# The small constant of sixty softmax sums: added by VectorE in front of its reciprocal instead of by ScalarE

## The chip, the cores and the metric

The kernel runs on one core of one Trainium2 chip. The metric is the device time of one launch in microseconds (us), given as the median of several runs of the same program.

## What is computed

A causal attention over 4 batches and 12 heads (448 positions, head dimension 64) is followed by a gated feed-forward block with an RMS norm in front of it. Cut to what matters here:

```
scores = q @ k^T / 8, causal mask, minus the row maximum
attn   = exp(scores)
attn   = attn / (sum(attn) + 1e-9)          # this sum and this 1e-9
x      = attn @ v                           # heads side by side, 1792 tokens by 768
xn     = x / sqrt(mean(x * x) + 1e-6) * g
out    = (silu(xn @ w_gate) * (xn @ w_val)) @ w_out
```

## The kernel before

The attention is cut into 60 units: a pair of heads (one head on each half of the partitions) times a block of queries. The first 12 units (kind 0) have 256 queries as two blocks, so each has four softmax sums per partition; the other 12 of the first two groups look the same, and the last 36 (kinds 1 and 2) have two sums per partition. The feed-forward block runs in between: its matmuls for the first groups of tokens lie among the attention's steps, so that TensorE has work while a softmax is under way.

Each engine works through its own instructions in the order in which the program was written. That order comes from a hand-made clock: `tick()` counts steps, `post(delay, fn)` writes an instruction so many steps later, and the table `T` holds the delays. Nothing is moved by a scheduler, so an instruction that waits holds everything behind it on its engine.

One unit p goes through these steps:

- **Scores** (L193): TensorE multiplies queries and keys into a PSUM bank.
- **Masked maximum** (L202): VectorE adds the mask, scales, writes the tile `sp` and gets the row's extreme `nm`. That is one custom instruction and one that reads its accumulator, for each head and block.
- **Exponential** (L205): ScalarE takes exp of `sp` in place and gets the row sum `sm` through its accumulator.
- **The constant** (L227): one ScalarE Identity with a bias tile `tiny` of 1e-9 adds the constant to all two or four sums of the unit in place.
- **Reciprocal** (L214, in `norm`): VectorE writes `rs` from `sm`. A pair of units that is treated in one round has its two reciprocals side by side.
- **Normalization** (L210 on GpSimd, called POOL in the profile; L208 on ScalarE for units 10 to 23): `sp` times `rs`.
- **Transposes** (L249) by TensorE, **copies** to `pt` (L253 by VectorE, L255 by ScalarE), and the **product with v** (L275) by TensorE into `a_ps`, which L292 copies out.

Between these, VectorE and ScalarE also prepare the weights of the feed-forward block. ScalarE scales a weight tile (L414) and rounds it to a high part `w_h` (L429); VectorE puts together bit fields (L417 and then L419, which reads what L417 wrote) and takes the low part `w_l` (L431). Later VectorE forms sums of weight tiles (L450). POOL takes a share of this too (L415, L103).

Of the kernel before, what the change touches and what calls it, by code (L numbers as in the profile page):

```python
# [10 lines left out]
F32 = mybir.dt.float32  # L11
# [4 lines left out]
AF = mybir.ActivationFunctionType  # L16
# [6 lines left out]
P = 128  # L23
# [15 lines left out]
        for g in range(NG) for c in range(NP)}  # L39
ENDS = [max(i for i, u in enumerate(UNITS) if u[0] == g) + 1 for g in range(NG)]  # L40
# [3 lines left out]
T = dict(c0=0, c1=1, c10=5, c2=4, c20=16, c3=4, c30=18, c26=5, c36=5, c5=6, c50=19, c56=7, exp=1, exp0=3, gt=1, hh=1, hl=4, ws=5, ld2=7,  # L44
         ld=4, ld1=11, lv=5, norm0=7, norm1=2, r0=1, acc=10, acc4=7, dg=1, spread=2, r1=5, so=3, wl=2, wl0=7, wl2=5, wl4=1, xl=2, xl0=9)
# [17 lines left out]
def attention_ffn(ctx: ExitStack, tc: tile.TileContext, qk0, qk1, qk2, v, v2, w, g, out, out2):  # L63
# [7 lines left out]
    nc = tc.nc  # L71
# [3 lines left out]
    def pool(name, bufs, at=ctx, **kw):  # L75
        return at.enter_context(tc.tile_pool(name=name, bufs=bufs, **kw))

    const = pool("const", 1, side="left")
# [15 lines left out]
    def bank(tag, bufs=1):  # L94


        return ps.tile([P, W], F32, tag=tag, name=tag + "_ps", bufs=bufs)
# [22 lines left out]
    nc.vector.memset(ones, 1.0)  # L120
    eps = const.tile([P, 1], F32, name="eps")
    nc.vector.memset(eps, 1e-6)
    tiny = const.tile([P, 1], F32, name="tiny")
    warm_up = const.tile([P, 1], F32, name="warm_up")
    nc.vector.memset(tiny, 1e-9)
    g_sb = const.tile([P, KD], F32, name="g_sb")


# [3 lines left out]
    def post(delay, fn):  # L132
        if delay <= 0:
            fn()
        else:
            later.setdefault(now[0] + delay, []).append(fn)
# [14 lines left out]
    def load_qk(p):  # L151
        if p < len(UNITS):
            _, kind, _, _, row, _ = UNITS[p]
            raw_qk[p] = raw.tile([P, 2, W], F32, tag="qk", name="qk_r")
            if kind == 2:
                nc.sync.dma_start(out=raw_qk[p], in_=qk2[row])
            else:
                nc.sync.dma_start(out=raw_qk[p][:, 0], in_=(qk0, qk1)[kind][row])
# [10 lines left out]
    def blocks(kind):  # L169

        return [(0, P), (P, 2 * P)] if kind == 0 else [(0, KEYS[kind])]

    def steps_s(p):


        if not 0 <= p < len(UNITS):
            return []
        _, kind, _, _, _, _ = UNITS[p]
        pr = hs[p] = dict(norms=[])
        bl = blocks(kind)  # L180
        nb = 2 * len(bl)

        def scores(pss):
            for i, (o, wd) in enumerate(bl):
                for h in range(1 + (kind == 2)):
                    for e in range(2):
                        r = raw_qk[p][e * D: (e + 1) * D, h]
                        if kind == 2:
                            ps, q0, nq = pss[e][h * D: (h + 1) * D, :wd], 0, D
                        else:  # L190
                            ps, q0, nq = pss[e][:, o: o + wd], i * P, P
                        k0 = nq if kind else 2 * P
                        nc.tensor.matmul(ps, r[:, q0: q0 + nq], r[:, k0: k0 + wd],  # L193
                                         start=True, stop=True)

        def softmax(e, i, pss):
            o, wd = bl[i]
            ps, sp = pss[e][:, o: o + wd], pr["sp"][e][:, o: o + wd]
            n = len(bl) * e + i
            nm, sm, rs = (pr[m][:, n: n + 1] for m in ("nm", "sm", "rs"))  # L200
            mk = mask2 if kind == 2 else mask[:, 3 * P - wd:]
            nc.vector.tensor_tensor_reduce(  # L202
                out=sp, in0=ps, in1=mk, scale=nsc, scalar=3.0e38,
                op0=ALU.add, op1=ALU.min, accum_out=nm)
            post(T["exp" if p >= ENDS[0] else "exp0"], lambda: nc.scalar.activation(  # L205
                sp, sp, AF.Exp, bias=nm, scale=-1.0, accum_out=sm))
            if ENDS[0] - 2 <= p < ENDS[1]:
                pr["norms"].append(lambda: nc.scalar.mul(sp, sp, rs))  # L208
            else:
                pr["norms"].append(lambda: nc.gpsimd.tensor_scalar(  # L210
                    sp, sp, rs, 1.0, op0=ALU.mult, op1=ALU.mult))

        def norm():
            nc.vector.reciprocal(pr["rs"][:, :nb], pr["sm"][:, :nb])  # L214
            post(2 if ENDS[0] - 2 <= p < ENDS[0] else 0, lambda: [f() for f in pr["norms"]])

        def step():
            for nm in ("nm", "sm", "rs"):
                pr[nm] = st_p.tile([P, 4], F32, tag=nm, name=nm)
            pr["sp"] = [sp_p.tile([P, S], F32, tag="sp", name="sp") for _ in range(2)]  # L220
            pss = [bank(t_) for t_ in "xy"] if p > ENDS[1] + DP and p % 2 == 0 else [
                bank("s", 2) for _ in range(2)]
            scores(pss)
            for e in range(2):
                for i in range(len(bl)):
                    softmax(e, i, pss)
            post(T["exp" if p >= ENDS[0] else "exp0"], lambda: nc.scalar.activation(  # L227
                pr["sm"][:, :nb], pr["sm"][:, :nb], AF.Identity, bias=tiny))
            post(T["norm1" if kind else "norm0"], norm)
            post(2, lambda: load_qk(p + 4))  # L230

        return [step]
# [602 lines left out]
    with tc.manual_schedule():  # L835
# [157 lines left out]
        for q in range(21):  # L993
            i, p = divmod(q, 3)
# [58 lines left out]
```

## Time and profile before

| | |
|---|---|
| Median of 3 runs | 682.22 us (682.05 to 683.24) |
| The profiled execution | 681.84 us, of which the span of all instructions is 680.0 us |
| TensorE (PE) busy | 667.7 us, 98% of the span |
| VectorE (DVE) busy | 535.2 us, 79% |
| ScalarE (ACT) busy | 378.3 us, 56% |
| GpSimd (POOL) busy | 287.7 us, 42% |
| Granted TensorE clock | 1.00 in every stretch, which is the upper of its two levels |

Busy times are sums over instructions. The shares are averages over stages that differ much: in the first 50 us attention runs almost alone, from 68 us on the feed-forward matmuls fill TensorE, and from 428 us on there is no attention any more. The durations of neighbouring VectorE or ScalarE instructions overlap a little in the records, so the distance from one start to the next says what an instruction costs its engine. In the rows, "idle" is the time an engine stood still in front of an instruction, and the name behind the arrow is what ended it.

### The profile page before, as it was taken

The page shows a single profiled execution, that of the slowest core. Times are in us where ns is not written, and L with a number is a line of the kernel's source. Part 1 is how long each engine was busy: PE and PEld are TensorE (multiplying, and loading weights), DVE is VectorE, ACT ScalarE, POOL GpSimd, SP SyncE. Part 2 cuts the span into 40 slices and gives each one's busy share as a digit, 9 for nine tenths or more (in the row PEclk, how much of TensorE's full clock was granted, in tenths as well). Part 3 has the DMA queues.
Part 4 walks back from the last instruction along what each step waited for, and adds up shares of the span by engine and source line. Part 5 has one row for each costly group of instructions (what it writes and reads, how often), then busy time and mean ns, then how long its engine had stood idle before and what let it go on. Part 6 is the DMA issues. An engine that isn't in the chain of part 4 may idle for free.

```text
span 680.0 us, 11926 instructions
## 1 busy us (share of the span) xinstructions
PE 667.7 (98%) x4116; PEld 550.8 (81%) x4116; DVE 535.2 (79%) x1059; ACT 378.3 (56%) x855; POOL 287.7 (42%) x262
## 2 busy tenths in 40 slices
PE   8989999999999999999999999999999999999997
PEld 5566877777777767777777777888999999999997
DVE  4998998999888486877777878487577866889982
ACT  6986779787876444545545353434534343355540
POOL 4971121222235427565765665563333342402220
PEclk9999999999999999999999999999999999999999
DMA  8765788787977556777667645316775457563541
GB/s 269 243 235 189 230 244 291 230 262 242 283 260 283 164 159 233 216 242 207 228 213 239 208 159 182 122 62 197 250 242 178 161 194 240 196 172 89 155 140 59
DMA packets 71356, 138.81 MB, mean 204 GB/s; under 512 B 7744, under 2 KB 39232, under 8 KB 71296
## 3 DMA queue, kind: packets, MB, share of 16 engines
q1 hardware_dynamic: 71296, 138.05, 63.0%
q8 instruction: 33, 0.54, 0.3%
q14 instruction: 27, 0.22, 0.1%
HBM read 104.21 MB, written 33.82 MB: 203 GB/s over the span
## 4 chain that ended last, share of the span: by engine, by line
PE 68%; DVE 1%; ACT 1%; DMA 0%; issue 0%; SPq 0%; DVEq 0%; ACTq 0%
PE s_ps L625 10%; PE m_ps L475 9%; PE m_ps L625 9%; PE m_ps L477 9%; PE m_ps L476 9%; PE y_ps L625 5%; PE a_ps L275 5%; PE x_ps L625 4%; PE t_ps L249 4%; PE s_ps L193 2%; PE x_ps L193 2%; DVE w_r L450 1%; DMA w_o<-wsum 0%; ACT sp L205 0%; ACT w_c L414 0%
## 5 line engine op out<-in xcount | busy, mean ns | idle before, releaser
L475 PE MATMUL m_ps<-xh,w_h 128*128 128x512 f32 x276 | 117.3, 425 | 0.0
L210 POOL TENSOR_SCALAR sp<-sp,rs 128x384 f32<-128x384 f32 (+2 forms) x112 | 77.7, 711 | 90.7 <-DVE rs L214 86.1
L205 ACT ACTIVATE sp<-sp,nm 128x384 f32<-128x384 f32 (+3 forms) x168 | 87.1, 521 | 41.3 <-DVE nm L202 41.3
L477 PE MATMUL m_ps<-xh,w_l 128*128 128x512 f32 x276 | 108.4, 393 | 0.0
L476 PE MATMUL m_ps<-xl,w_h 128*128 128x512 f32 x276 | 108.3, 392 | 0.0
L415 POOL TENSOR_SCALAR w<-w 128x768 f32<-128x768 f32 x36 | 39.8, 1108 | 104.4 <-ACT w_c L414 98.3
L103 POOL TENSOR_TENSOR a_l<-w_q,a_h 128x768 fp32r<-128x768 f32 x24 | 48.2, 2007 | 81.0 <-ACT a_h L516 81.0
L275 PEld LDWEIGHTS a_ps<-pt,v_r 128*64 128x64 f32 (+1 forms) x864 | 42.1, 137 | 31.9 <-issue 9.7
L275 PE MATMUL a_ps<-pt,v_r 128*64 128x128 f32 (+2 forms) x864 | 58.5, 268 | 6.0 <-DVE pt L253 3.2
L103 POOL TENSOR_TENSOR w_l<-w_r,w_h 128x768 fp32r<-128x768 f32 x30 | 59.5, 1992 | 6.2 <-ACT w_h L429 6.0
L475 PEld LDWEIGHTS m_ps<-xh,w_h 128*128 128x128 f32 x276 | 51.9, 188 | 11.8 <-issue 3.7
L477 PEld LDWEIGHTS m_ps<-xh,w_l 128*128 128x128 f32 x276 | 51.9, 188 | 11.8
L253 DVE COPY pt<-t_ps 128x384 f32<-128x384 f32 (+1 forms) x71 | 42.4, 597 | 23.9 <-PE t_ps L249 23.5
L475 PE MATMUL m_ps<-hh,w_h 128*128 128x512 f32 x144 | 58.6, 407 | 0.0
L202 DVE CUSTOM_DVE_ANT_0 sp<-s_ps,mask 128x128 f32<-128x128 f32 (+3 forms) x136 | 49.7, 414 | 10.9 <-PE s_ps L193 9.9
L476 PEld LDWEIGHTS m_ps<-xl,w_h 128*128 128x128 f32 x276 | 52.2, 189 | 7.6
L477 PE MATMUL m_ps<-hh,w_l 128*128 128x512 f32 x144 | 56.3, 391 | 0.0
L476 PE MATMUL m_ps<-hl,w_h 128*128 128x512 f32 x144 | 56.2, 390 | 0.0
L249 PE MATMUL t_ps<-ident,sp 128*128 128x128 f32 (+1 forms) x309 | 50.1, 275 | 0.1
L249 PEld LDWEIGHTS t_ps<-ident,sp 128*128 128x128 f32 (+1 forms) x309 | 37.9, 138 | 14.3 <-issue 2.0
L193 PE MATMUL s_ps<-qk_r 64*128 64x128 f32 (+3 forms) x296 | 42.6, 425 | 0.5 <-DVE nm L202 0.4
L516 ACT CAST a_h<-w_q 128x768 fp32r<-128x768 f32 (+1 forms) x48 | 35.0, 754 | 14.1 <-DMA w_q<-wz 4.3
(194 smaller groups left out, 1667.9 us busy)
## 6 DMA issues: line engine op xcount, KB each, us to landing
w<-in_w SPq DMA_DIRECT2D x36, 768.0 KB, 5.7
w<-w_c SPq DMA_DIRECT2D x36, 384.0 KB, 5.8
w_r<-w SPq DMA_DIRECT2D x36, 384.0 KB, 4.5
qk_r<-in_qk SPq DMA_DIRECT2D x48, 256.0 KB, 4.6
qk_r<-in_qk SPq DMA_DIRECT2D x12, 512.0 KB, 5.7
v_r<-in_v SPq DMA_DIRECT2D x12, 448.0 KB, 4.8
v_r<-in_v SPq DMA_DIRECT2D x24, 192.0 KB, 3.0
wy<-w_r SPq DMA_DIRECT2D x24, 192.0 KB, 4.3
```

The source lines that it names most:

```text
L103: nc.gpsimd.tensor_tensor(out_, a, b, op=op)
L193: nc.tensor.matmul(ps, r[:, q0: q0 + nq], r[:, k0: k0 + wd], start=True, stop=True)
L202: nc.vector.tensor_tensor_reduce(out=sp, in0=ps, in1=mk, scale=nsc, scalar=3.0e38, op0=ALU.add, op1=ALU.min, accum_out=nm)
L205: post(T["exp" if p >= ENDS[0] else "exp0"], lambda: nc.scalar.activation(sp, sp, AF.Exp, bias=nm, scale=-1.0, accum_out=sm))
L210: pr["norms"].append(lambda: nc.gpsimd.tensor_scalar(sp, sp, rs, 1.0, op0=ALU.mult, op1=ALU.mult))
L249: nc.tensor.transpose(ps[:kb, at: at + P], pr["sp"][e][:, o + kb * j: o + kb * (j + 1)], ident)
L253: nc.vector.tensor_copy(pt[:kb, :at], ps[:kb, :at])
L275: nc.tensor.matmul(av_ps[e * D: (e + 1) * D, p % 2, q0: q0 + n], raw_v[p][:kb, h, j, e, :], pr["pt", e][:kb, a0: a0 + n], start=(j == 0), ...
L475: nc.tensor.matmul(ps, wh[:, k, :], mh, start=(first and k == ks[0]), stop=False)
L476: nc.tensor.matmul(ps, wh[:, k, :], ml, start=False, stop=False)
L477: nc.tensor.matmul(ps, wl[:, k, :], mh, start=False, stop=(last and k == 5))
L625: nc.tensor.matmul(ps, a[x], b[y], start=first and n == 0, stop=last and n == 2, skip_group_check=True)
```

## The change

The Identity on ScalarE goes away, with its bias tile `tiny` and the memset that fills it. In its place `norm` begins with a VectorE instruction that writes `sm + 1e-9` to `rs`, and the reciprocal then reads `rs` and writes it again in place.

```
-    tiny = const.tile([P, 1], F32, name="tiny")
     warm_up = const.tile([P, 1], F32, name="warm_up")
-    nc.vector.memset(tiny, 1e-9)
...
         def norm():
-            nc.vector.reciprocal(pr["rs"][:, :nb], pr["sm"][:, :nb])
+            nc.vector.tensor_scalar_add(pr["rs"][:, :nb], pr["sm"][:, :nb], 1e-9)
+            nc.vector.reciprocal(pr["rs"][:, :nb], pr["rs"][:, :nb])
...
-            post(T["exp" if p >= ENDS[0] else "exp0"], lambda: nc.scalar.activation(
-                pr["sm"][:, :nb], pr["sm"][:, :nb], AF.Identity, bias=tiny))
```

On VectorE, in the stretch of kind 0 units, this stood behind the maxima of one unit before (square brackets name the engines whose semaphores the instruction waits for, here Activation for ScalarE and DVE for VectorE itself):

```order
L202 ISA nm 128x1
L214 RECIPROCAL rs<-sm 128x4 [waits Activation_49]
L292 COPY xr<-a_ps 128x256 [waits PE_49]
L431 TENSOR_TENSOR w_l<-w_c,w_h 128x768 [waits Activation_49]
L253 COPY pt<-x_ps 128x384 [waits PE_49]
```

With the change the same place reads as follows, with line numbers that are lower by two or three:

```order
L200 ISA nm 128x1
L212 TENSOR_SCALAR rs<-sm 128x4 [waits Activation_49]
L213 RECIPROCAL rs<-rs 128x4 [waits DVE_49]
L289 COPY xr<-a_ps 128x256 [waits PE_49]
L428 TENSOR_TENSOR w_l<-w_c,w_h 128x768 [waits Activation_49]
L250 COPY pt<-x_ps 128x384 [waits PE_49]
```

The wait for ScalarE moved to the added instruction, and the reciprocal now waits for VectorE's own instruction in front of it. The order of all the rest is the same on VectorE.

On VectorE, in the rounds of two units late in the attention, two reciprocals stood side by side before:

```order
L253 COPY pt<-t_ps 112x512 [waits PE_49]
L214 RECIPROCAL rs<-sm 128x2 [waits Activation_49] x2
L502 TENSOR_TENSOR t_sb<-t_sb,m_ps 128x512 [waits PE_49]
L253 COPY pt<-t_ps 112x512 [waits PE_49]
L450 TENSOR_TENSOR w_r<-w_r 128x384 [waits DMAHW2_49,DVE_49]
```

With the change there are four small instructions, each reciprocal behind the add that it needs:

```order
L250 COPY pt<-t_ps 112x512 [waits PE_49]
L212 TENSOR_SCALAR rs<-sm 128x2 [waits Activation_49]
L213 RECIPROCAL rs<-rs 128x2 [waits DVE_49]
L212 TENSOR_SCALAR rs<-sm 128x2 [waits Activation_49]
L213 RECIPROCAL rs<-rs 128x2 [waits DVE_49]
L499 TENSOR_TENSOR t_sb<-t_sb,m_ps 128x512 [waits PE_49]
```

There are 16 such pairs and 28 single places, 60 adds in all, and 60 Identities and one memset fewer. The orders of TensorE, of POOL and of the queue that issues the transfers are the same as before.

## Rows read from the trace of the kernel before

**Rows 1.** Busy time of each engine by stretch (us, instructions in brackets).
```profile
core 0: us, PE busy (x) PEld busy (x) DVE busy (x) ACT busy (x) POOL busy (x), PEclk, DMA share, GB/s
17.00:51.00 34.00, 30.29 (x205) 19.63 (x204) 33.05 (x103) 31.90 (x103) 28.67 (x37) 1.00 0.70 239
...
68.00:402.00 334.00, 333.56 (x2171) 252.18 (x2169) 273.66 (x584) 207.63 (x507) 150.05 (x139) 1.00 0.72 232
...
428.00:605.00 177.00, 177.00 (x956) 167.52 (x955) 126.44 (x189) 71.88 (x124) 69.88 (x42) 1.00 0.56 185
```

**Rows 2.** Waits of TensorE: us in total, times, longest.
```profile
PE a_ps L275 <- DVE pt L253: 3.2, 6, 1.3
PE a_ps L275 <- DMA v_r<-in_v: 1.8, 2, 1.0
...
PE a_ps L275 <- ACT pt L255: 0.9, 4, 0.3
```

**Rows 3.** Groups of ScalarE: busy us, mean ns, idle before.
```profile
L227 ACT ACTIVATE sm<-sm,tiny 128x2 f32<-128x2 f32 (+1 forms) x60 | 17.8, 297 | 1.9
```

**Rows 4.** Timeline of ScalarE around one Identity: start us, duration us.
```profile
22.64 0.19 ACT L205 ACTIVATION_READ_ACCUMULATOR sp<-sp,nm 128x1 f32 x1
22.74 0.50 ACT L205 ACTIVATE sp<-sp,nm 128x256 f32<-128x256 f32 x1
23.14 0.19 ACT L205 ACTIVATION_READ_ACCUMULATOR sp<-sp,nm 128x1 f32 x1
...
23.56 0.82 ACT L429 CAST w_h<-w_c 128x768 fp32r<-128x768 f32 x1
```

**Rows 5.** Small VectorE instructions, groups by shape: busy us, mean ns.
```profile
L214 DVE RECIPROCAL rs<-sm 128x2 f32<-128x2 f32 x36 | 4.1, 150 | 3.9 <-ACT sm L227 3.9
...
L358 DVE TENSOR_SCALAR dg<-ident,rc 128x128 f32<-128x128 f32 x4 | 0.9, 283 | 0.1
...
L122 DVE MEMSET eps<- 128x1 f32 x1 | 0.1, 59 | 0.0
```

**Rows 6.** Timeline of VectorE, an instruction and one that reads its result.
```profile
59.75 0.95 DVE L417 SCALAR_TENSOR_TENSOR w<-w 128x768 int32<-128x768 int32 x1
60.73 0.96 DVE L419 SCALAR_TENSOR_TENSOR w_c<-w_c,w 128x768 int32<-128x768 int32 x1
```

**Rows 7.** Timeline of VectorE, 14 to 50 us, idle time in square brackets.
```profile
14.83 0.18 DVE L214 RECIPROCAL rs<-sm 128x4 f32<-128x4 f32 x1 [1.48 <-ACT sm L227]
...
17.28 0.18 DVE L214 RECIPROCAL rs<-sm 128x4 f32<-128x4 f32 x1 [0.40 <-ACT sm L227]
...
20.62 0.18 DVE L214 RECIPROCAL rs<-sm 128x4 f32<-128x4 f32 x1 [0.25 <-ACT sm L227]
...
28.03 0.17 DVE L214 RECIPROCAL rs<-sm 128x4 f32<-128x4 f32 x1
...
49.23 0.96 DVE L431 TENSOR_TENSOR w_l<-w_c,w_h 128x768 fp32r<-128x768 f32 x1 [0.41 <-ACT w_h L429]
```

**Rows 8.** Reciprocals from 20.6 to 49 us: durations, first and last start.
```profile
L214 DVE RECIPROCAL rs<-sm x8: 161/166/179, 20.6 to 48.3; 128x4 f32<-128x4 f32 x8
```

**Rows 9.** Timeline of TensorE where it stood still for a copy.
```profile
54.03 1.31 PE L275 MATMUL a_ps<-pt,v_r 128*64 128x256 f32 x8 [0.20 <-ACT pt L255]
...
107.39 0.86 PE L275 MATMUL a_ps<-pt,v_r 128*64 128x256 f32 x6 [0.18 <-ACT pt L255]
...
200.02 0.86 PE L275 MATMUL a_ps<-pt,v_r 128*64 128x256 f32 x6 [0.25 <-ACT pt L255]
...
414.64 0.87 PE L275 MATMUL a_ps<-pt,v_r 128*64 128x128 f32 x10 [0.48 <-DVE pt L253]
```

**Rows 10.** Chain that ended last, two stretches: start us, us on the chain.
```profile
192.16 0.10 DVE rs L214
...
197.39 0.03 ACT sm L227
...
408.55 0.14 DVE rs L214 x2
```

**Rows 11.** Timeline of POOL.
```profile
27.66 1.03 POOL L103 TENSOR_TENSOR sq<-xr 128x512 f32<-128x512 f32 x1
```

## The prediction

> **What bounds the kernel now.** I read the busy time by stretch first. From 428 us on TensorE has no gap and there is no softmax left, so nothing of the change can act there except by shifting the whole tail [rows 1]. From 68 to 402 us TensorE works 333.56 of 334.00 us, while VectorE is free for 60.3 us and ScalarE for 126 us [rows 1]. From 17 to 51 us it is otherwise: VectorE is busy for 33.05 of 34 us, ScalarE for 31.90, and TensorE stands still for 3.7 us [rows 1]. So I looked at TensorE's waits next. It waits 3.2 us for copies that VectorE makes of transposed weights of attention, in 6 places, and 0.9 us for those of ScalarE [rows 2]. A change that touches VectorE and ScalarE can move the end only where TensorE stands still for one of them, and TensorE's gaps then say by how much. They lie in three places: the stretch up to 54 us, two single gaps of 0.18 and 0.25 us at 107 and 200 us, and one of 0.48 us at 414.6 us [rows 9]. The chain that ended last agrees for the last two: it goes through VectorE's reciprocals at 192.16 and 408.55 us and through one Identity at 197.39 us [rows 10].
>
> **What the removal gives.** 60 Identities of 297 ns go, 17.8 us of busy time [rows 3]. On its engine one costs less or more than its duration, so I take distances between starts: from the last accumulator read to the next work is 0.42 us with an Identity between (23.14 to 23.56), and 0.10 us without (22.64 to 22.74), which makes 0.32 us [rows 4]. The sum itself is ready about 0.33 us sooner: the read at 23.14 ends at 23.33, and with the Identity the result would come at some 23.66 us (23.56, its successor's start, plus the 0.10 us by which neighbours overlap). The memset of 59 ns runs once, before TensorE has scores [rows 5].
>
> **What the addition costs.** The trace has no VectorE add on four columns, so I bound it. The reciprocal on two columns takes 150 ns, a scalar operation on 128 columns 283 ns, and a memset of one column 59 ns [rows 5]. The add is nearest to the reciprocal: same input memory, same output, as few columns. I take 0.15 us, with 0.06 and 0.28 us as ends. The reciprocal must now wait until the add is finished. What such a wait adds is shown by L417 and L419: the first ends at 60.70 us and the second, which reads its result, starts at 60.73 us, so 0.03 us [rows 6]. One add thus costs VectorE S = 0.18 us in front of the reciprocal, with bounds of 0.09 and 0.31 us. Nothing behind the reciprocal changes.
>
> The Trainium skill, "VectorE: DVE Perf Modes", section on the TRN2 errata, gives 58 cycles plus the columns for an operation from SBUF to SBUF, which would make an estimate of 0.06 us for the add, S = 0.09 us, and a sum at the low end below; the same section says that its own measurements have a fixed part of about 150 cycles, an estimate of 0.16 us. By the reciprocal's 150 ns the trace agrees with the second.
>
> **First place, up to 54 us: +0.34 us.** Three reciprocals stand behind ScalarE: VectorE waits 1.48, 0.40 and 0.25 us at 14.83, 17.28 and 20.62 us [rows 7]. There the add lies partly in time that was lost anyway. Each such place gains 0.33 - 0.18 = 0.15 us at most; three in a row could add up to 0.45 us, but the gain is cut where the copies behind them wait for transposes, so I take 0.30 us in the middle. From 20.6 us on VectorE works without a gap until 48.8 us. Eight reciprocals lie there, the first being the one just counted [rows 8]. The other seven put 7 x 0.18 = 1.26 us in front of everything behind them: the copy of `a_ps`, the work on weights, and the copy L253 for which TensorE waits. That leaves VectorE 1.26 - 0.30 = 0.96 us late. At 49.23 us it stood 0.41 us waiting for `w_h` from ScalarE [rows 7], and ScalarE, which there has one Identity less in front of it, doesn't get later by as much; the wait takes up 0.41 us, and 0.55 us is left. At 54.03 us TensorE had waited 0.20 us for a copy by ScalarE [rows 9]; that takes up 0.20 us more. Left: 0.34 us. With S = 0.31 the three places give nothing, seven adds cost 2.17 us, and 1.56 us is left. With S = 0.09 VectorE is 0.50 us ahead after the third place, pays 0.63 us, and the rest is decided by ScalarE's own chain, which has lost an Identity: about -0.25 us. TensorE's two waits for `v_r`, 1.8 us [rows 2], lie in the same stretch; they could swallow a gain, not a loss, since the copies arrive about when these transfers do.
>
> **Second place, 107 and 200 us: -0.30 us.** The ScalarE work that ends in the copy has one Identity in it and one reciprocal ahead of it (192.16 and 197.39 us in the second case [rows 10]). Each gives 0.18 - 0.33 = -0.15 us, which both gaps have room for [rows 9]. Bounds: -0.42 us, where the first gap is used up, and -0.04 us.
>
> **Third place, 408 to 415 us: +0.36 us.** The pair of reciprocals at 408.55 us lies on the chain [rows 10]; behind it come the evicted product, a tanh on ScalarE, weight sums and the copy for which TensorE waits at 414.64 us [rows 9]. Two adds make 0.36 us (0.18 to 0.62), and that gap grows by it.
>
> **Everywhere else: 0.** Of the 48 adds after 64 us, 8.6 us of work, all but the few above fall into VectorE's 60.3 us of free time [rows 1]. Where that cover fails, a pair costs TensorE 0.36 us. ScalarE's 15 us of saved work there fall into its 126 us of free time.
>
> **The sum.** 0.34 - 0.30 + 0.36 = +0.40 us, between -0.5 and +2.1 us. On the profiled execution this makes 682.24 us (681.84 + 0.40). The median of the runs shown is 0.38 us above that execution, so the forecast for a median is 682.22 + 0.40 = 682.6 us. A measurement of this kernel can tell about 0.2%, 1.36 us, from no change, so this is no change.
>
> **Rival: VectorE's add waits for POOL, slower.** If the add may not run while POOL is in an instruction of its own, VectorE stands still until POOL is through. The reciprocal at 28.03 us shows what is at stake: POOL runs from 27.66 to 28.69 us [rows 7, 11], so an add there would start 0.66 us late. POOL is busy for 28.67 of the 34 us [rows 1]. Were six of the nine adds from 17 us on caught, each for some 0.5 us, 3.0 us would come on top: 685.6 us. It decides as soon as two or three adds are caught. For it: VectorE has no gap there that could cover it. Against it: a scalar operation on 128 columns takes only 133 ns more than a reciprocal on two [rows 5], which is near one column a cycle, so the form seen here doesn't seem to run in a faster mode.
>
> The Trainium skill, "SBUF — State Buffer", section "Who interferes with whom", has the rule behind this: a scalar operation on VectorE can enter a mode that uses two ports, one pair of which it shares with GpSimd, and then whichever comes second waits for the whole instruction. By that rule the time would be the 685.6 us above if the mode is entered, and the forecast's if not; no row here shows the add's mode.
>
> **Rival: ScalarE sets the pace up to 50 us, faster.** If the two engines run in step because VectorE's work waits on ScalarE's, then eight rounds give 0.32 us each: -2.6 us in the first place, -2.5 us in all, 679.7 us. For it: three waits of VectorE for an Identity, and ScalarE busy for 31.90 of 34 us [rows 1, 7]. Against it: behind 20.62 us the reciprocals never wait again, as only the first of the eight in that stretch has a wait.
>
> That the change doesn't do what it says is excluded by the order of instructions: the Identities are gone and the adds stand in front of the reciprocals.
>
> **How the numbers follow.** The forecast has a chance of 0.72, the wait for POOL 0.15, ScalarE's pace 0.07, and 0.06 is for a loss beyond 1.36 us without POOL: S at its upper end (+2.1 us), or a few more pairs that are not covered. Faster by over 0.2%: 0.07. Within: 0.72. Slower: 0.15 + 0.06 = 0.21. The range goes from 681.5 us (the sum's low end, 681.7, and a spread of the runs) to 684.6 us (its high end, 684.3, and the same); it leaves out the faster case and most of the wait for POOL.
>
> **What would show it.** In the profile after, the distance from the start of an add to that of its reciprocal should be 0.18 us; much more, and unequal, where POOL is at work means the first rival. VectorE's waits before the sums at 14.8 to 20.6 us should be shorter by about 0.3 us each, TensorE's gaps at 107 and 200 us nearly closed, that at 414.6 us about 0.8 us. TensorE should come to its first work after 54 us some 0.3 us later than before. If it gets there over 1 us earlier, ScalarE set the pace and the prediction is wrong; if over 1.5 us later, the adds cost more than any small row of the trace says.

## The result, and the profile after

The changed kernel takes 685.39 us (median of 6 runs, 685.07 to 686.5), the kernel before 682.13 us beside it (6 runs, 679.74 to 683.24). The ratio is 1.0062, with an interval of [1.0048, 1.0076]: slower, by 3.3 us from median to median and by some 4 us by the ratio. The prediction said 682.6 us, in a range from 681.5 to 684.6 us. The time lies above that range, and beside the 685.6 us of the first rival, the wait of VectorE's add for POOL.

The profiled execution took 686.02 us, its span 684.2 us. First the busy time by stretch, with the same columns as [rows 1]:

```profile
17.00:51.00 34.00, 29.88 (x190) 18.71 (x191) 33.73 (x112) 26.96 (x88) 29.80 (x41) 0.95 0.58 198
68.00:402.00 334.00, 333.64 (x2169) 251.67 (x2168) 281.06 (x630) 197.51 (x465) 149.93 (x133) 1.00 0.73 232
```

From 17 to 51 us ScalarE has 4.94 us less to do than in [rows 1] and VectorE 0.68 us more, and TensorE starts 190 matmuls in place of 205. The stretch holds less work and VectorE is as full as before, so something in it takes VectorE's time without doing work. The add shows what. This is the view of its line: minimum, median and maximum in ns.

```profile
L212 DVE TENSOR_SCALAR rs<-sm x60: 147/158/880, 8.5 to 424.5; 128x2 f32<-128x2 f32 x36, 128x4 f32<-128x4 f32 x24
```

The median is what the prediction assumed; the maximum is 5.6 times that. Two of the adds in VectorE's timeline (start, duration), one of each kind:

```profile
31.00 0.70 DVE L212 TENSOR_SCALAR rs<-sm 128x4 f32<-128x4 f32 x1
31.74 0.18 DVE L213 RECIPROCAL rs<-rs 128x4 f32<-128x4 f32 x1
...
36.27 0.16 DVE L212 TENSOR_SCALAR rs<-sm 128x4 f32<-128x4 f32 x1
36.46 0.18 DVE L213 RECIPROCAL rs<-rs 128x4 f32<-128x4 f32 x1
```

And POOL's timeline around the first of them, which answers to [rows 11]:

```profile
30.64 1.04 POOL L103 TENSOR_TENSOR sq<-xr 128x512 f32<-128x512 f32 x1
32.11 2.83 POOL L208 TENSOR_SCALAR sp<-sp,rs 128x128 f32<-128x128 f32 x4 [0.43 <-DVE rs L213]
```

The add starts at 31.00 us, while POOL is in its square, and ends at 31.70; the square ends at 31.68. The add at 36.27 us falls into a pause of POOL and takes 0.16 us. Six of the 60 adds end with a POOL instruction in this way: at 18.38 us (0.88), 22.33 (0.69), 26.60 (0.56), 31.00, 40.27 and 49.54 us (0.70 each). Over 0.155 us each that is 3.3 us. Two more, at 10.52 and 148.27 us, meet only the end of a POOL instruction and take 0.25 and 0.27 us. Behind the add at 31.00 us POOL stands still for 0.43 us as well, because its next work needs the reciprocal. TensorE's waits, to be read against [rows 2]:

```profile
PE a_ps L272 <- DVE pt L250: 4.8, 8, 0.9
PE a_ps L272 <- DMA v_r<-in_v: 2.7, 1, 2.7
...
PE t_ps L246 <- POOL sp L208: 0.5, 1, 0.5
```

The waits for VectorE's copy of transposed attention weights grow from 3.2 to 4.8 us, five of them of 0.67 to 0.92 us between 29 and 52 us, and a wait for POOL's normalised scores is new. The wait for `v_r` is a single one of 2.66 us at 17.21 us. In other executions such waits come at other units (0.73 and 1.02 us in [rows 2]; 2.22 us at 23.15 us in one kernel below), and three kernels below with the same six stretched adds (e5, e9, e10) have at most 0.34 us of it in their first 40 us, while e6 and e8, without a stretched add, have 2.22 and 1.69 us. So I take it as chance and don't count it to the change.

### The profile page after: what moved, and what is told of

The parts are those of the page before. It is cut to its first block, busy times and chain, and to the rows that moved or that the text cites. A ratio compares the mean times of both kernels' runs of the same rounds, so it can differ in the third digit from the quotient of the medians.

```text
span 684.2 us, 11971 instructions
## 1 busy us (share of the span) xinstructions
PE 669.5 (98%) x4116; PEld 549.9 (80%) x4116; DVE 547.1 (80%) x1118; ACT 361.1 (53%) x795; POOL 290.9 (43%) x262
## 4 chain that ended last, share of the span: by engine, by line
PE 89%; DVE 7%; DMA 1%; issue 1%; ACT 1%; SPq 0%; DVEq 0%; ACTq 0%
PE m_ps L472 14%; PE m_ps L474 14%; PE m_ps L473 13%; PE s_ps L622 10%; PE m_ps L622 9%; PE a_ps L272 6%; PE y_ps L622 5%; PE x_ps L622 4%; PE t_ps L246 4%; PE s_ps L191 4%; PE x_ps L191 2%; DVE sp L200 1%; DMA w<-in_w 1%; DVE pt L250 1%; DVE w_r L447 1%
## 5 line engine op out<-in xcount | busy, mean ns | idle before, releaser
L208 POOL TENSOR_SCALAR sp<-sp,rs 128x384 f32<-128x384 f32 (+2 forms) x112 | 80.5, 736 | 96.1 <-DVE rs L212 63.8
L412 POOL TENSOR_SCALAR w<-w 128x768 f32<-128x768 f32 x36 | 41.8, 1162 | 102.2 <-ACT w_c L411 90.5
L272 PE MATMUL a_ps<-pt,v_r 128*64 128x128 f32 (+2 forms) x864 | 60.7, 269 | 8.4 <-DVE pt L250 4.8
L103 POOL TENSOR_TENSOR w_l<-w_r,w_h 128x768 fp32r<-128x768 f32 x30 | 58.0, 1941 | 6.0 <-ACT w_h L426 5.8
L473 PE MATMUL m_ps<-hl,w_h 128*128 128x512 f32 x144 | 56.2, 390 | 0.0
```

The source lines that it names most:

```text
L103: nc.gpsimd.tensor_tensor(out_, a, b, op=op)
L208: pr["norms"].append(lambda: nc.gpsimd.tensor_scalar(sp, sp, rs, 1.0, op0=ALU.mult, op1=ALU.mult))
L272: nc.tensor.matmul(av_ps[e * D: (e + 1) * D, p % 2, q0: q0 + n], raw_v[p][:kb, h, j, e, :], pr["pt", e][:kb, a0: a0 + n], start=(j == 0), ...
L473: nc.tensor.matmul(ps, wh[:, k, :], ml, start=False, stop=False)
```

## A clock for the places

Sums of waits say nothing of where the time is lost for good. For that I use the starts of TensorE's products `a_ps`: unit 3, unit 11 (the last of the first place), unit 15, unit 22 and the last one. The distances in us, from the timelines of TensorE (e1 to e14 are the experiments):

```
kernel                      3 to 11   11 to 15   15 to 22   22 to last
before                       32.42      76.39      80.36      212.17
changed                      35.21      76.65      79.70      213.19
e1  no 1e-9                  32.26      76.17      79.50      211.99
e2  60 reductions            33.05      79.34 c    79.50      214.15
e3  60 adds, pointer         35.52      78.09      79.79      214.86
e4  12 adds, 48 Identities   33.70 v    76.33      80.18      212.24
e5  12 adds                  35.42      75.88      79.50      212.08
e6  12 reductions            30.91 v    76.10      79.50      212.11
e7  48 adds                  32.22      78.19      79.50      213.14
e8  48 Identities            32.25      76.62      79.48      212.23
e9  60 adds, two tensors     35.27      76.63      79.40      213.29
e10 60 copies                35.41      77.92      79.74      213.15
e11 changed, POOL has less   33.44 v    77.97      79.50      213.16
e12 changed, POOL has least  31.64 v    78.19 c    79.49      213.25
e13 e1 without POOL's w      31.29      75.33      79.50      212.00
e14 e7 without POOL's w      31.32      75.32      79.50      213.20
v: unit 3 itself had waited 0.8 to 2.2 us; c: the clock had fallen (last section)
```

Changed against before: +2.79, +0.26, -0.66 and +1.02 us, 3.4 us together. The stretched add at 18.38 us lies ahead of unit 3 and can add up to 0.7 us that the table doesn't show; in e5, against e1, unit 3 comes 0.31 us later (22.10 against 21.79 us). Behind the last product nothing of the change is left. The spans of the two profiles, 684.2 and 680.0 us, differ by more than the 3.4 us: unit 3 comes 2.3 us later in the changed kernel, behind the wait for `v_r`, and the work behind the last product took 1.4 us longer in the execution of before (257.0 against 255.6 us).

## The experiments

**e1: no 1e-9.** The add is gone, and the Identity isn't put back.

```diff
-nc.vector.tensor_scalar_add(pr["rs"][:, :nb], pr["sm"][:, :nb], 1e-9)
-nc.vector.reciprocal(pr["rs"][:, :nb], pr["rs"][:, :nb])
+nc.vector.reciprocal(pr["rs"][:, :nb], pr["sm"][:, :nb])
```

> This kernel leaves the 1e-9 out altogether: neither the Identity nor the add; the reciprocal reads the sums as before. Theory A (the add waits until POOL's running instruction ends) and theory B (each add and the wait of its reciprocal simply cost a packed VectorE some 0.2 us or more, whatever POOL does) both expect that the loss is gone and that TensorE's gaps at 107 and 200 us close: 0.4 to 0.6 us under the kernel before, about 681.6 us, ratio 0.999. Theory C (the loss comes from taking work from ScalarE: everything ahead of the first weight tile runs sooner, and transfers at the start collide, as ScalarE's wait of 2.57 us for a weight tile at 13.5 us suggests) expects a loss of 1.4 us or more over the kernel before, 683.5 to 685 us.

679.48 us, ratio to before 0.9963 [0.995, 0.9975]: faster than both kernels, and by more than expected. In the table, before loses 0.22 us to it from unit 11 to 15 and 0.86 us from 15 to 22, the places of the two single gaps in [rows 9]. The rest of the difference in the profiles, 1.1 us, lies in the last 60 us, where TensorE did 115 matmuls per 20 us in before's execution (620 to 660 us) and 117 to 118 in this one; the granted clock is given as 1.00 in both, nothing of the change reaches there, and the cause stays open. Theory C, by which the loss came from taking work from ScalarE, is out: that work is gone here too, and the time is lower. Each sum holds the exponential of the row's own maximum, so it is at least 1, and an fp32 number of that size doesn't change when 1e-9 is added to it; this kernel computes the same.

**e2: a reduction over an axis of one element in place of the add.** It has VectorE do as small an instruction at the same place, with the same dependence.

```diff
-nc.vector.tensor_scalar_add(pr["rs"][:, :nb], pr["sm"][:, :nb], 1e-9)
+nc.vector.tensor_reduce(pr["rs"][:, :nb],
+    pr["sm"][:, :nb].rearrange("p (n o) -> p n o", o=1), axis=AxisListType.X, op=ALU.add)
```

> In place of the add stands a VectorE sum over an axis of one element, from sm to rs, 128 partitions by two or four; it leaves the 1e-9 out and costs VectorE one instruction and one wait of the reciprocal as the add does, but reads through another form. Theory A expects that this form does not wait for POOL: every one of the 60 takes about 0.15 us, and the time is that of the forecast, 682.4 to 682.8 us. Theory B expects the time of the changed kernel, 685.4 us. Theory C expects 685 us too.

684.61 us, 1.0038 [1.0026, 1.005]. The line of the reductions, and one of them in VectorE's timeline:

```profile
L212 DVE TENSOR_REDUCE rs<-sm x60: 132/145/157, 8.5 to 423.6; 128x2 f32<-128x2 f32 x36, 128x4 f32<-128x4 f32 x24
...
28.44 0.15 DVE L212 TENSOR_REDUCE rs<-sm 128x4 f32<-128x4 f32 x1
```

POOL at that time:

```profile
28.07 1.03 POOL L103 TENSOR_TENSOR sq<-xr 128x512 f32<-128x512 f32 x1
```

The reduction begins 0.37 us into POOL's square, as the add did in the changed kernel, and is done after 0.15 us. No reduction is stretched, though eight of the 60 begin inside a POOL instruction with more than 0.2 us of it left; the eight adds that do so in the changed kernel are the six and the two more named above. So the wait belongs to the form of the instruction, not to the place. The time was a miss: 2 us more than expected. From unit 3 to 11 the kernel loses only 0.8 us against e1, but 3.2 us from 11 to 15 (of which 1.2 us by a fall of the clock) and 2.2 us at the end, with a wait of 0.80 us for POOL's scores at 260.94 us that no other kernel has. What else costs it so much behind unit 11 is taken up with e7 and e14.

**e3: the 1e-9 as a pointer operand.** `tiny`, a tile of one column, stands in place of the number.

```diff
-nc.vector.tensor_scalar_add(pr["rs"][:, :nb], pr["sm"][:, :nb], 1e-9)
+nc.vector.tensor_scalar_add(pr["rs"][:, :nb], pr["sm"][:, :nb], tiny)
```

> The add takes its 1e-9 from a tile of one column per partition in place of a constant in the instruction; all else as in the changed kernel. Theory A leaves open whether this form is caught too. If it is not (the four scalar operations of L358, which take such an operand, ran at about one column a cycle), the adds take 0.15 to 0.2 us each and the time is 682.4 to 682.9 us; if it is, six adds are stretched to 0.5 to 0.9 us and the time is 685.4 us. Theories B and C expect 685.4 us.

687.97 us, 1.0088 [1.0075, 1.0101]. The adds take 0.22 us in the median and up to 0.88 us, the same six being stretched. A pointer doesn't avoid the wait and costs 0.06 us more each. The time is 2.6 us above what was expected; the table puts 1.4 us of that, against the changed kernel, from unit 11 to 15 (see e7) and 1.7 us at the end.

**e4: adds in the first 12 units, Identities in the other 48.**

```diff
+if p < ENDS[0]:
     nc.vector.tensor_scalar_add(pr["rs"][:, :nb], pr["sm"][:, :nb], 1e-9)
     nc.vector.reciprocal(pr["rs"][:, :nb], pr["rs"][:, :nb])
+else:
+    nc.vector.reciprocal(pr["rs"][:, :nb], pr["sm"][:, :nb])
...
+if not (p < ENDS[0]):
+    post(..., lambda: nc.scalar.activation(sm, sm, AF.Identity, bias=tiny))
```

> Only the first 12 units have the add on VectorE; the other 48 keep the Identity on ScalarE. Theory A expects nearly the whole loss here, since the six adds that were stretched lie in these units: 3 to 3.5 us over the kernel before, 685.2 us, with TensorE's gaps at 107 and 200 us as before. Theory B expects at most 12 x 0.22 = 2.6 us less the 0.6 us that the forecast found to be taken up, 684 us. Theory C expects 684 to 685 us.

684.66 us, 1.0041 [1.0028, 1.0054]. Twelve adds of the 60 bring about two thirds of the loss. That lies between the 684 us of theory B and the 685.2 us of theory A, so the time doesn't separate them. In its trace five of the twelve are stretched, to 0.54 to 0.79 us, and TensorE's two gaps are there as expected (0.22 us at 110.05 and 0.13 us at 202.47 us).

**e5 to e8: one part alone.** e5 is e4 without the Identities, e6 has the reduction of e2 in the first 12 units, e7 the adds in the other 48, e8 the Identities in these 48; elsewhere the sums go to the reciprocal as they are, as in e1. The edit is the condition of e4, or its opposite:

```diff
-if p < ENDS[0]:
+if p >= ENDS[0]:
```

> The 1e-9 is added on VectorE in the first 12 units only; in the other 48 it is left out, without any instruction in its place. The kernel without any 1e-9 took 679.5 us. Theory W (VectorE's add waits for POOL): six adds of 0.5 to 0.9 us again lie in the first 12 units and put 3.3 us in front of TensorE, which the last product of these units should show against the kernel without 1e-9; 682.9 us, ratio to before 1.002. Theory V (each instruction more on VectorE costs the same 0.1 us, POOL or not, over all 60 units): 1.2 us, 680.7 us, ratio 0.998.

> As the kernel with adds in the first 12 units only, but with a reduction over a one-element axis in place of each add (it copies the sums, so 1e-9 is left out everywhere). Theory W: reductions of 0.15 us, none stretched, and 1.0 us for the 12 of them, as in the first 12 units of the kernel with 60 reductions: 680.5 us, ratio 0.998, over 2 us below the kernel with adds there. Theory V: 680.7 us as well, but with the kernel with adds at the same time.

> The 1e-9 is added on VectorE in the last 48 units only; in the first 12 it is left out, without any instruction in its place. Theory W: no add waits for POOL there (0.15 to 0.17 us each), and only the units from 350 to 420 us lose something, 0.9 us, as they did in the changed kernel: 680.4 us, ratio 0.998. Theory V: 48 of 60 parts of 5.9 us, 4.7 us: 684.2 us, ratio 1.0036.

> The 1e-9 is added by ScalarE's Identity in the last 48 units only; in the first 12 it is left out. Theory R (the Identity costs TensorE its two waits at 107 and 200 us, with what follows each, 0.58 and 0.87 us in the kernel before against the kernel without 1e-9): 1.4 us over the kernel without 1e-9, 680.9 us, ratio 0.9987, and both waits are there. Rival (what the kernel without 1e-9 gains comes from the first 12 units, where three reciprocals wait for an Identity): 679.5 us, ratio 0.996.

e5: 683.71 us, 1.0038 [1.0025, 1.0051]. e6: 679.93 us, 0.9987 [0.9976, 0.9997]. The same dependence at the same place costs 3.8 us more as an add than as a reduction, and theory V (each instruction more costs the same) has it at nothing: V is out. In the traces e5's unit 11 comes at 57.52 us and e6's at 54.06 us, against 54.05 us in e1; what theory W foresaw as 3.3 us for the adds is 3.47 us, and its 1.0 us for the reductions is not to be seen there. The ratios lie about 1.6 us higher against e1 than the traces do, in both; that stays open.

e7: 681.78 us, 1.001 [1.0001, 1.0019], and it fits neither theory. No add is stretched beyond 0.27 us, yet 2.0 us go from unit 11 to 15 and 1.15 us at the end. Where the first part goes, TensorE shows, in two waits for ScalarE's copy:

```profile
107.57 0.43 PE L275 MATMUL a_ps<-pt,v_r 128*64 128x256 f32 x2 [0.24 <-ACT pt L255]
...
121.27 0.43 PE L275 MATMUL a_ps<-pt,v_r 128*64 128x256 f32 x2 [0.88 <-ACT pt L255]
```

With what follows each, they put TensorE 0.7 and 1.3 us behind e1. Ahead of the longer one stands this instruction on VectorE, in e7 and then at the same place in e1:

```profile
109.47 1.63 DVE L431 TENSOR_TENSOR w_l<-w_c,w_h 128x768 fp32r<-128x768 f32 x1
```

```profile
108.49 0.96 DVE L427 TENSOR_TENSOR w_l<-w_c,w_h 128x768 fp32r<-128x768 f32 x1
```

and POOL beside it, again in e7 and then in e1:

```profile
109.21 1.08 POOL L415 TENSOR_SCALAR w<-w 128x768 f32<-128x768 f32 x1 [4.13 <-ACT w_c L414]
```

```profile
108.77 1.42 POOL L411 TENSOR_SCALAR w<-w 128x768 f32<-128x768 f32 x1 [3.20 <-ACT w_c L410]
```

In e1 the subtraction `w_l` comes first, takes 0.96 us, and POOL's instruction is the one that lasts longer. In e7 POOL comes first by 0.26 us and `w_l` takes 1.63 us, 0.67 us more, and the maxima, scores and reciprocals behind it come later. But `w_l` starts 0.98 us later than in e1 to begin with. An add had turned the order at the `w_l` before it, which ends in the wait at 107.57 us. VectorE and POOL there, in e7 and then in e1:

```profile
104.26 1.63 DVE L431 TENSOR_TENSOR w_l<-w_c,w_h 128x768 fp32r<-128x768 f32 x1
...
104.20 0.88 POOL L415 TENSOR_SCALAR w<-w 128x768 f32<-128x768 f32 x1 [4.60 <-DVE rs L213]
```

```profile
103.89 0.93 DVE L427 TENSOR_TENSOR w_l<-w_c,w_h 128x768 fp32r<-128x768 f32 x1
...
104.05 1.52 POOL L411 TENSOR_SCALAR w<-w 128x768 f32<-128x768 f32 x1 [4.58 <-DVE rs L212]
```

In e7 the add at 103.97 us stands right ahead of this `w_l` and puts it 0.20 us back, so that it starts 0.06 us behind POOL instead of 0.16 us ahead of it. So an instruction that was there before the change pays for an add that isn't stretched itself. Of the 14 kernels down to e12 in the table, the five with a long `w_l` (1.62 or 1.63 us) at the later place (e2, e3, e7, e10, e11), which are also the five with a long one at the earlier (1.58 to 1.66 us), lose 1.7 us or more from unit 11 to 15 against e1; of the others only e12 does, whose clock fell.

e8: 680.95 us, 1.0003 [0.9989, 1.0016]. Theory R is half right. The Identities cost 0.45 us at the first of the two places, with a wait of 0.21 us at 108.15 us; the second gap, at 200 us, isn't there, while e4 has it with 0.13 us. It needs the first place's delay of before or something else that I didn't isolate.

**e9: the add with two tensors.** **e10: a copy in place of the add.**

```diff
-nc.vector.tensor_scalar_add(pr["rs"][:, :nb], pr["sm"][:, :nb], 1e-9)
+nc.vector.tensor_tensor(pr["rs"][:, :nb], pr["sm"][:, :nb], tiny[:, :nb], op=ALU.add)   # e9
+nc.vector.tensor_copy(pr["rs"][:, :nb], pr["sm"][:, :nb])                               # e10
```

> The 1e-9 is added as a tensor of four columns that is filled once, by a VectorE operation with two inputs in SBUF. Theory W1 (a VectorE operation waits for POOL whenever it has two inputs there as well, as the Trainium skill's page SBUF - State Buffer has it): adds of 0.5 to 0.9 us again in the first 12 units, the last product of unit 11 at 57 to 59 us, 685 to 686 us. Theory W2 (only the form with one tensor and a number waits): all adds near 0.16 us, the last product of unit 11 at 54 to 55 us as with reductions, 684 us or less.

> A copy of the four sums in place of the add; the 1e-9 is left out. Theory W1 (any VectorE operation from SBUF to SBUF with one tensor as input waits for POOL, reductions excepted): copies of 0.5 to 0.9 us at the six places, unit 11's product at 57 to 59 us, 685 to 686 us. Rival (it is the scalar of the add that makes it wait): copies below 0.2 us, unit 11's product at 54 to 55 us, 684 us or less.

e9: 684.6 us, 1.0054 [1.0032, 1.0075]. e10: 683.56 us, 1.004 [1.0021, 1.006]. Both lie below the 685 to 686 us that theory W1 had, so the durations have to decide. The lines of both, e9 first:

```profile
L214 DVE TENSOR_TENSOR rs<-sm,tiny x60: 140/152/766, 8.5 to 421.4; 128x2 f32<-128x2 f32 x36, 128x4 f32<-128x4 f32 x24
```

```profile
L212 DVE COPY rs<-sm x60: 147/158/784, 8.8 to 423.4; 128x2 f32<-128x2 f32 x36, 128x4 f32<-128x4 f32 x24
```

Theory W1 in both: the same six places, 0.53 to 0.78 us, and 35.3 and 35.4 us from unit 3 to 11 as in the changed kernel. The number in the add has no part in it. Unit 11's product came at 56.2 and 56.7 us, somewhat ahead of the 57 to 59 us expected, since these executions had no early wait for `v_r`.

The Trainium skill, "SBUF — State Buffer", section "Who interferes with whom", has it so: on VectorE scalar operations and copies contend with GpSimd in the mode that uses both port pairs, an operation with two inputs in SBUF contends with a GpSimd instruction that reads SBUF, and a reduction never does. The six places in e9 and e10, and their absence in e2, agree with all three; no run here shows the mode itself, and by its rule the changed kernel's time would be the rival's 685.6 us, and 685.39 us was measured.

**e11 and e12: less work for POOL.** e11 is the changed kernel without POOL's multiplication L412 (by 0.0 and then by 1.0; the expectations name it by its last factor) for the five weights of the first 12 units. L412 is a step of the weights' conversion, which e11 and e12 leave out for these weights and e13 and e14 for all. In e12 ScalarE makes POOL's squares in the first 12 units as well.

```diff
-(T["c1" if s > 4 else "c10"], lambda: nc.gpsimd.tensor_scalar(
+(T["c1" if s > 4 else "c10"], lambda: s > 4 and nc.gpsimd.tensor_scalar(
     hf_, hf_, 0.0, 1.0, op0=ALU.mult, op1=ALU.mult)),
...
-if b or c == NP - 2:
+if b or c <= NP - 2:        # e12 alone
     nc.scalar.activation(sq, x, AF.Square)
```

> The changed kernel, where the multiplication by one that POOL applies to the weights' upper halves is left out for the five weights converted in the first 12 units (0.9 us of POOL each). Theory W: adds that fell into it are back at 0.16 us, so that of the six stretched ones only those in POOL's squares stay; the last product of unit 11 comes about 1.2 us earlier than in the changed kernel's kind of execution (56 to 57.5 us), and the time is about 684.2 us. Rival (the adds are stretched by something else that comes at the same moment, a transfer or ScalarE's accumulator): still six, time as changed, 685.4 us.

> As the kernel with fewer POOL instructions, and the squares of the first 12 units made by ScalarE. POOL has only the multiplications by the reciprocals left there, for which it needs the add's result. Theory W: no add above 0.2 us, the last product of unit 11 at 54 to 55.5 us, and a time of 682 to 683 us, since 3.3 us of waiting are gone and ScalarE gets 2.5 us of work. Rival as before: six stretched adds and 685.4 us or more.

e11: 682.79 us, 1.0028 [1.0013, 1.0043]. e12: 682.15 us, 1.0008 [0.9991, 1.0024]. The adds of e11, then of e12:

```profile
L212 DVE TENSOR_SCALAR rs<-sm x60: 148/158/694, 8.8 to 421.1; 128x2 f32<-128x2 f32 x36, 128x4 f32<-128x4 f32 x24
```

```profile
L212 DVE TENSOR_SCALAR rs<-sm x60: 148/158/273, 8.3 to 420.7; 128x2 f32<-128x2 f32 x36, 128x4 f32<-128x4 f32 x24
```

In e11 those over 0.3 us are four: 0.45 us at 19.59 and 0.69 us at 27.61, 36.48 and 45.35 us, in POOL's squares. In e12 there is none, and unit 11's product comes at 53.89 us, as in the kernels without adds there. With the instruction of POOL the stretch of VectorE's add goes: the wait is POOL's. The ratio goes from 1.0062 to 1.0028 and 1.0008, but not all of that need be the adds': e11 came out 1.4 us faster than expected, and e13, which has no add at all, gets unit 11's product at 52.19 us in place of e1's 54.05 us by the lack of L412 alone.

**e13 and e14: e1 and e7 without L412 for any weight.**

```diff
-(T["c1" if s > 4 else "c10"], lambda: nc.gpsimd.tensor_scalar(
-    hf_, hf_, 0.0, 1.0, op0=ALU.mult, op1=ALU.mult)),
```

> The kernel without any 1e-9, where POOL's multiplications of the weights' upper halves are left out for all converted weights (0.9 us of POOL each, part of the weights' conversion). It is the base for the next kernel. Theory W2 (in the last 48 units it is the subtraction w_l, of two tensors in SBUF and there before the change, that is stretched from 0.96 to 1.63 us when it comes second to POOL): no w_l above 1.1 us between 60 and 200 us, and unit 15's product 75.5 to 76.3 us after that of unit 11 (76.2 us in the kernel without 1e-9). Rival (the 1.63 us come from something else): w_l of 1.63 us remain.

> The kernel with adds in the last 48 units only, and likewise without POOL's multiplications of the weights' upper halves. Theory W2: unit 15's product comes at most 0.6 us later behind that of unit 11 than in the base without POOL's multiplications (in the kernels with them the adds made it 2.0 us later), TensorE's wait of 0.88 us at 121 us is gone or below 0.4 us, and the time is 1.0 to 2.0 us over that base. Rival (the adds delay ScalarE's multiplications by themselves, without POOL): still 2.0 us later with a wait of 0.8 us or more.

e13: 677.72 us, 0.9936 [0.991, 0.9961]. e14: 678.37 us, 0.9945 [0.9927, 0.9964]. The line of `w_l` in e14:

```profile
L429 DVE TENSOR_TENSOR w_l<-w_c,w_h x36: 925/948/959, 23.7 to 220.2; 128x768 fp32r<-128x768 f32 x36
```

None is above 0.96 us, and from unit 11 to 15 the 48 adds cost nothing: 75.32 against 75.33 us, where they had cost 2.0 us with POOL's instruction, and neither of the two waits of e7 is left. That loss was POOL's too. What stays is 1.20 us from unit 22 to the last, which L412 has no part in; its place is shown under the third place below. The time lies 0.65 us above e13's, less than the 1.0 to 2.0 us expected, and e13's 75.33 us from unit 11 to 15 just below the 75.5 to 76.3 us.

## Why the prediction was wrong, step by step

**What the removal gives, and what an add costs.** Both sizes were right where nothing interferes. An add takes 0.15 to 0.16 us and its reciprocal starts 0.19 us behind it (36.27 to 36.46 us); S was 0.18 us. VectorE's early waits went another way than foretold: the first add waits 2.77 us at 16.20 us for ScalarE in an execution with late transfers, the next two not at all.

**First place: this step failed.** The prediction took S for each of the adds there and had TensorE 0.34 us late at its first work behind 54 us. It was 2.8 us later from unit 3 on alone (3.5 us at unit 11 in e5 against e1, without an early wait for `v_r`), because the adds that met POOL's longer instructions cost 0.56 to 0.88 us; that is beyond the 1.5 us that the prediction itself had named as the sign of a dearer add. (Its remainder of 0.34 us is 0.35 us by its own terms, which changes nothing.) The price had been read from the reciprocal, which isn't stretched in any trace here, also where it falls into a POOL instruction: the row of 28.03 us [rows 7] beside [rows 11] shows that, and I used it only to say where an add would wait. What the prediction said against the rival, that a scalar operation doesn't seem to run in a faster mode, was no argument: the add with two tensors of e9 waits as well.

The trace before could have told. `w_l`, two tensors in SBUF, comes in two lengths there, and the longer beside POOL. The line of it, and one of the longest:

```profile
L431 DVE TENSOR_TENSOR w_l<-w_c,w_h x36: 916/951/1654, 24.6 to 224.0; 128x768 fp32r<-128x768 f32 x36
...
119.91 1.65 DVE L431 TENSOR_TENSOR w_l<-w_c,w_h 128x768 fp32r<-128x768 f32 x1
```

```profile
119.39 1.36 POOL L415 TENSOR_SCALAR w<-w 128x768 f32<-128x768 f32 x1 [2.57 <-DVE w_c L419]
```

It starts 0.52 us into POOL's instruction and lasts 0.7 us longer than the median. A maximum 1.7 times the median in a group of one shape was the row to look for.

**Second place: the sum was right, its parts were not.** The two gaps at 107 and 200 us are gone, as foretold, and from unit 11 to 22 the changed kernel is 0.40 us faster (predicted 0.30). But closing the second gap gives 0.66 us, more than the 0.25 us of the gap and above the bound that I took from it, and at the first place it loses 0.26 us. Which of the two engines wins at `w_l` decides whether this place gains 0.4 us or loses 0.9 us (e7, 157.69 against 156.75 us).

**Third place: right in place, and three times too small.** The prediction had one gap grow by 0.36 us. That gap fell from 0.48 to 0.41 us, and two new waits came ahead of it:

```profile
387.63 0.55 PE L272 MATMUL a_ps<-pt,v_r 128*64 128x128 f32 x6 [0.34 <-DVE pt L250]
...
415.75 0.52 PE L246 MATMUL t_ps<-ident,sp 128*128 128x128 f32 x3 [0.50 <-POOL sp L208]
```

In all it is 1.02 us (212.17 to 213.19), and 1.1 to 1.3 us in e7, e9, e10, e11, e12 (against e1) and e14 (against e13), with stretched adds or without. The pair of adds delays POOL's multiplication of the scores. At 415.75 us TensorE waits for that directly. At 387.63 us it waits for a copy of VectorE, and ahead of that copy stands one more instruction with two tensors as input, before and then changed, each with POOL's subtraction beside it:

```profile
377.80 1.60 DVE L494 SCALAR_TENSOR_TENSOR t_sb<-t_sb,gr 128x512 f32<-128x512 f32 x1 [0.29 <-ACT t_sb L493]
...
377.00 1.85 POOL L103 TENSOR_TENSOR w_l<-w_r,w_h 128x768 fp32r<-128x768 f32 x1
```

```profile
382.58 1.97 DVE L491 SCALAR_TENSOR_TENSOR t_sb<-t_sb,gr 128x512 f32<-128x512 f32 x1 [0.30 <-ACT t_sb L490]
...
382.17 1.84 POOL L103 TENSOR_TENSOR w_l<-w_r,w_h 128x768 fp32r<-128x768 f32 x1
```

The same instruction takes 0.68 us at 377.90 us of the changed kernel, where POOL stands still. It begins 0.41 us into POOL's in place of 0.80 us and lasts 0.38 us longer, and likewise in e7 and e14 (1.97 and 1.98 us, against 1.62 and 1.60 us in e1 and e13). So the wait for POOL has a part here too, though no add is stretched; no run takes it away alone. The prediction had looked at one place, and at no wait for POOL.

**Everywhere else.** Right: from 15 to 22 the 48 adds of e7 cost nothing, and behind 428 us nothing is left.

**The rivals.** The wait for POOL was the case, with six adds caught, as its price had assumed, and for 0.40 to 0.73 us each beyond their own 0.155 us. Its chance of 0.15 was too small. That its 685.6 us comes so near the 685.39 us is partly luck: the six were assumed, and the other terms of the sum were off by 0.1 us less and 0.7 us more. ScalarE doesn't set the pace: without any 1e-9 the first place is 0.16 us faster, not 2.6 us.

## What to carry to other kernels

Before an instruction is moved to VectorE, look at what GpSimd does at that moment: an instruction of 0.16 us can cost the rest of a 1 us instruction of the other engine, and a delay of 0.2 us can make another instruction, which had always come first, come second. Whether that is so here can be read from the trace of the kernel before, in the spread of durations of one shape and in what POOL does at the start of the long ones; a price taken from an instruction of another kind doesn't hold it. The best answer here was to ask whether the instruction is needed: without the 1e-9, which changes no sum of at least 1, the kernel takes 0.9963 of the time before.

## What the runs showed of the hardware that was not expected

- The wait goes both ways, and the first to start keeps its length: `w_l` 0.96 or 1.63 us, POOL's L411 1.42 us where it comes second and 0.89 to 0.90 us where nothing is in its way. The recorded starts don't settle a tie: in the changed kernel `w_l` begins 0.04 us behind POOL at 109.22 us and keeps its 0.93 us. It doesn't depend on the size: adds of four columns wait as the subtraction of 768 columns does, reductions and reciprocals of the same four columns don't.
- TensorE's clock fell in the profiled executions of e2 and e12 and not in that of e1, though the same work stood there. Three of the eleven executions of the kernel before beside e1 have a mean clock of 0.997 too, so the fall doesn't need the change. In e2, in the columns of [rows 1]:

```profile
56.00:59.00 3.00, 2.87 (x21) 2.22 (x19) 2.52 (x4) 0.98 (x2) 1.65 (x2) 1.00 0.97 329
59.00:63.00 4.00, 4.00 (x12) 2.77 (x11) 3.22 (x8) 0.26 (x1) 0.00 (x0) 0.57 0.07 21
```

The granted clock was 0.57 over these 4 us, most of them at the lower of its two levels (1.2 of 2.4 GHz), and the matmul of 512 columns took 0.63 in place of 0.40 us. Ahead of the fall TensorE had done 16 matmuls of one column each, with three of 512 columns between them (56.26 to 59.2 us). It costs these two kernels 1.2 us between unit 11 and 12. In the changed kernel's profile the clock is 0.95 from 17 to 51 us, behind the wait of 2.66 us. Single profiles differ by such a microsecond, which is why the distances between products were read rather than the spans.
